# Attention and MoE in one kernel: the order of an attention unit's work on four engines taken from a table of beats

## The chip, the core and the metric

The kernel runs on one NeuronCore of a Trainium2 chip. Its engines each have an in-order queue of their own: PE (TensorE, matrix products), DVE (VectorE), ACT (ScalarE), POOL (GpSimd) and SP (SyncE, which here only issues DMAs). The metric is the device time of one launch in microseconds (us).

## What is computed

```python
scores = scale * q @ k.T                      # (4, 8, 576, 576), head_dim 64
x = log1p(abs(pos_i - pos_j)) / log1p(max(pos_i, 1))
bias = relu(x[..., None] @ w1 + b1) @ w2       # hidden 32, 8 heads
a = scores + bias - max
a = exp(a); a = a / (a.sum(-1) + 1e-9)
x = (a @ v).transpose(0, 2, 1, 3).reshape(2304, 512)
h = x @ w_in                                   # 512 x 2048
g = where(h >= 1, h, where(h <= -1, 0, (h + 1)**2 / 4))
out = g @ w_out
```

Everything is fp32. The kernel gets that precision from products of a high part (a value rounded to fp32r) and a low part (the rest): of each product of two matrices it keeps high x high, low x high and high x low.

## The kernel before

There are three stages. The first builds the bias, 36 groups of 16 query rows, and writes it to DRAM (`steps`, `sums`, `combine`). The third is the MoE part, three blocks of 768 tokens, which waits for hardly anything but PE. Between them lies the attention, which the change is about.

**A unit** is one batch element and one pair of heads: 4 pairs x 4 batch elements make 16 units, n = 0 to 15. Queries come in four blocks of 128 (k = 0 to 3) and a last one (L) that holds the remaining 64 queries of both heads. For each block:

- PE computes scores S for both heads (12 products, line 429) into two PSUM tiles of two banks each. The pool `psS` has two such tiles, so the tiles of one block must be read before the next block's products can start.
- DVE adds the bias, negates and finds the row extreme in one instruction per head, written to e (line 457, 475 for L); this frees S.
- ACT takes the exponential in place and leaves the row sum in `sum` (line 464).
- PE transposes e in 128 x 128 pieces (line 432) into a PSUM tile T; tiles T come from a pool of four (`psT`), which also holds the outputs O and R.
- The transposed tile is split into hi and lo. Plain tiles: ACT rounds to hi, DVE subtracts for lo (lines 493, 494). For five of the eight tiles of a unit (`POOL` in `CFG`) ACT copies T to SBUF (c, line 498), hi is made by DVE from T (three of them, line 502) or by POOL from c (two, line 500), and POOL subtracts (line 503). Keys 512 to 575 of both heads share a tile (T_s, `shared`).
- PE multiplies the values by hi (5 products) and by lo (5 products) into O (line 429, `values`), ACT copies O out, SP stores it.

The row sums go: ACT adds eps, DVE takes the reciprocal of the 128 x 9 tile `sum` (line 629), PE transposes it into a tile R of its own (line 542), ACT copies it out (line 544), SP stores it. The reciprocals multiply x later, when the MoE part's activations are prepared.

**Preparation.** While unit n runs, unit n+1's q, k and v are loaded and split: DVE rounds kh (line 163) and vs (line 174), POOL subtracts (line 136). The pool of vs has two tiles, so vs of unit n+1 is written over that of unit n-1. Some units also prepare an activation tile of the first MoE block (`XQ`: load, add and multiply on DVE, lines 383 and 384, round on ACT, subtract on POOL) or a weight tile (`WQ`: units 5, 6, 9 and 10).

**The order** is that of the emitting loop: for each unit and block, the scores, a slot for preparation work (`step`), then an entry of `GAPS`, which holds transposes of the block before and output products of this unit or the one before:

```python
GAPS = (
    ((av, 1, 0, 1), (tr, 1, 4)),
    ((tr, 0, 0), (av, 1, 1, 0)),
    ((tr, 0, 1), (av, 1, 1, 1)),
    ((tr, 0, 2),),
    ((tr, 0, 3), (av, 0, 0, 0)),
)
```

`tr, 0, k` transposes block k of the current unit, `av, back, half, j` makes O of a unit `back` units earlier. Instructions that pass through `keep` stay in the order of the program on their engine; the others (most of DVE's and ACT's of the attention) a scheduler may move.

Of the kernel before, what the change touches and what calls it, by code (L numbers as in the profile page):

```python
# [32 lines left out]
CFG = dict(un=[('paaa', 'paav')[g in (1, 30, 32, 34)] for g in range(NG)], bb=5, mv=1, hi='pvvpv', rb='a', pool=((0, 1), (2, 0), (2, 1), (3, 0), (3, 1)), sb=4, keep=1, drain=2, diag='a', rb2='v', eps='v', rc=2, rbb=1, hb=2, rawb=(2, 2), t=(3, 11, 10, 18, 11, 12, 19), eb=4, seq=0, pb=(6, 9, 12, 14, 16), pq=22, tb=6, ub=12, low0='ppp', anch=(8, 8, 16, 23, 23), low1='ppp', ob=4, gb=4, fin=2, lastp=15, xs=2, sbf=('v', 'v', 'v', 'v', 'v'), bsE=(), ytail='p')  # L33
EPS = 1e-9
RB = 2
LASTP = CFG["lastp"]
FIRST = ((0, 3), (1, 5), (2, 33))
XQ = {(0, 0): (39, "raw", 43), (1, 0): (79, "raw", 83), (2, 0): (118, "raw", 123), (3, 0): (137, "bias", 142),
      (0, 1): (125, "x", 136), (1, 1): (131, "raw", 145), (2, 1): (139, "x", 151), (3, 1): (148, "raw", 155)}
WQ = {(0, 0): (49, 53), (0, 1): (59, 63), (1, 0): (89, 93), (1, 1): (99, 103)}  # L40
LB = ((1, 1), (2, 1), (3, 2), (3, 3), (2, 3))
POOL, SB, KEEP, RBB = CFG["pool"], CFG["sb"], CFG["keep"], CFG["rbb"]
STEPS = sorted((t, i) for i, t in enumerate(CFG["t"]))
# [5 lines left out]
def attn_cpb_moe_kernel(ctx, tc, qk, vL, cb, win, wout, lw, ident, ii, out):  # L49
# [27 lines left out]
    last_y, stored, narrow = [], [], []  # L77
# [71 lines left out]
    def prep(n):  # L149
# [4 lines left out]
        def high(ins):  # L154
            if n == 1:
                keep(ins)
            else:
                early(ins)
# [6 lines left out]
        def load_r():  # L165
            a["r"] = lp.tile([P, KQ], F32, tag="qk", name=f"qk{n}", bufs=CFG["rawb"][0])
            with ExitStack() as after:
                if n == 2:
                    after.enter_context(tc.issue_after(narrow[0].ins))
                nc.sync.dma_start(out=a["r"], in_=qk[n])  # L170
# [5 lines left out]
        def load_v():  # L176
            a["rv"] = lp.tile([P, 10, D], F32, tag="v", name=f"v{n}", bufs=CFG["rawb"][1])
            with ExitStack() as after:
                if n == 2:
                    after.enter_context(tc.issue_after(narrow[0].ins))  # L180
                nc.sync.dma_start(out=a["rv"].rearrange("p a b -> p (a b)"), in_=vL[n])

        def part(i):


            def f():
                if i == 0:
# [198 lines left out]
    def split_x(k, j, home):  # L386
# [15 lines left out]
        return scaled, high, rest  # L402

    with ExitStack() as ph:
# [8 lines left out]
        def load_bias(p, k):  # L413
# [8 lines left out]
            else:  # L422
                t = bp.tile([P, S], F32, tag="biasL", name=f"biasL{p}", bufs=2)
                for j in range(2):
                    narrow[:] = [nc.sync.dma_start(out=t[D * j : D * j + D, :], in_=bias_r[4][:, 2 * p + j, :])]
# [8 lines left out]
        def scores(n, k, qkv, bias):  # L434
            kh, kl = qkv["h"][:, :KW], qkv["l"][:, :KW]
            qh, ql = qkv["h"][:, KW:], qkv["l"][:, KW:]
            parts_ = ((qh, kh), (ql, kh), (qh, kl))
            if k == 0:
                sums[n] = stp.tile([P, 9], F32, tag="sum", name=f"sum{n}", bufs=3)
            later = []  # L440
            sm = sums[n]
            mx = stp.tile([P, 2], F32, tag="mx", name=f"mx{n}_{k}", bufs=6)
            if k < 4:
                e = ep.tile([P, 2 * S], F32, tag="e", name=f"e{n}_{k}")
                pss = [psS.tile([P, 2, 512], F32, tag="S", name=f"S{n}_{k}_{j}") for j in range(2)]
                for hf in range(2):
                    for i, (q_, k_) in enumerate(parts_):
                        for j in range(2):
# [3 lines left out]
                                pss[j][:, hf, :HS], q_[d, P * k : P * k + P], k_[d, kc : kc + HS],  # L452
                                start=i == 0, stop=i == 2, tile_position=(D * j, 0),
                            )
                for j, ps in enumerate(pss):
                    ev = e[:, S * j : S * j + S]
                    nc.vector.tensor_tensor_reduce(  # L457
                        out=ev.rearrange("p (a b) -> p a b", a=2),
                        in0=ps[:, :, :HS],
                        in1=bias[k][:, S * j : S * j + S].rearrange("p (a b) -> p a b", a=2),  # L460
                        scale=-0.125, scalar=BIG, op0=ALU.add, op1=ALU.min, accum_out=mx[:, j : j + 1],
                    )
                    later.append(
                        lambda ev=ev, j=j: nc.scalar.activation(  # L464
                            ev, ev, AF.Exp, bias=mx[:, j : j + 1], scale=-1.0, accum_out=sm[:, 4 * j + k : 4 * j + k + 1]
                        )
                    )
            else:
                e = ep.tile([P, S], F32, tag="eL", name=f"e{n}_L", bufs=2)
                ps = psS.tile([P, 2, 512], F32, tag="S", name=f"S{n}_L")  # L470
                for hf in range(2):
                    kc = D + HS * hf
                    for i, (q_, k_) in enumerate(parts_):
                        pe_mm(ps[:, hf, :HS], q_[:, 512:QW], k_[:, kc : kc + HS], start=i == 0, stop=i == 2)
                nc.vector.tensor_tensor_reduce(
                    out=e.rearrange("p (a b) -> p a b", a=2), in0=ps[:, :, :HS],
                    in1=bias[4].rearrange("p (a b) -> p a b", a=2),
                    scale=-0.125, scalar=BIG, op0=ALU.add, op1=ALU.min, accum_out=mx[:, 0:1],
                )
                def last():  # L480
                    y = nc.scalar.activation(e, e, AF.Exp, bias=mx[:, 0:1], scale=-1.0, accum_out=sm[:, 8:9])
                    for j in range(2):
                        h_ = slice(D * j, D * j + D)
                        nc.scalar.copy(diag[n % 2][h_, h_], e[h_, 512:S])
                    nc.scalar.activation(sm, sm, AF.Identity, bias=eps_s)
                    return y

                later.append(last)
            return e, later

        def split(ps, hi, lo, e=None, kj=None):
            if e is None:
                nc.scalar.copy(hi, ps)  # L493
                nc.vector.tensor_tensor(out=lo, in0=ps, in1=hi.bitcast(F32), op=ALU.subtract)  # L494
            else:
                c = sp.tile([P, 512], F32, tag="c4", name="c4", bufs=SB)
                m = c.rearrange("p (a b) -> p a b", a=4) if len(hi.shape) == 3 else c[:, : hi.shape[1]]
                nc.scalar.copy(m, ps)  # L498
                if CFG["hi"][POOL.index(kj)] == "p":
                    pool(nc.gpsimd.tensor_copy(hi, m))  # L500
                else:
                    nc.vector.tensor_copy(hi, ps)  # L502
                r = nc.gpsimd.tensor_tensor(out=lo, in0=m, in1=hi.bitcast(F32), op=ALU.subtract)  # L503
                pool(r)

        def EV(n, k, j):
            return nc.gpsimd if (k, j) in POOL and n < LASTP else None

        def transposes(n, k, es, eT):
            hi, lo = eT  # L510
            off = P * (k % 2)
            e = es[k]
            if k < 4:
                for j in range(2):
                    ps = psT.tile([P, 4, P], F32, tag="T", name=f"T{n}_{k}_{j}")
                    for tb in range(4):
                        c0 = 640 * j + P * tb
                        pe_tr(ps[:, tb, :], e[:, c0 : c0 + P], id_s)
                    split(ps, hi[:, 4 * j : 4 * j + 4, off : off + P], lo[:, 4 * j : 4 * j + 4, off : off + P], EV(n, k, j), (k, j))
            else:  # L520
# [26 lines left out]
        def values(n, half, j, eT, vs):  # L547
# [13 lines left out]
            if j == 0:  # L561
                return
# [521 lines left out]
```

## Time and profile before

| | us |
|---|---|
| median of 3 runs | 756.23 |
| range of the runs | 755.06 to 756.64 |
| the profiled execution | 756.44 |
| its span in the profile | 754.6 |
| PE busy | 703.7 (93% of the span) |
| DVE, ACT, POOL busy | 532.6, 518.3, 506.6 |
[...]

The span runs from the first to the last instruction; the execution's own time is 1.8 us more. PE counts as busy from a product's start to its modelled end, and products overlap in the pipeline, so a start-to-start distance says more than a sum of durations. A row of the timeline that merges several instructions gives the start of the first, the time to the end of the last and their count (x). What stands in brackets at a row's end is idle time just before it and what ended it.

### The profile page before, as it was taken

The numbers are of one execution on the slowest core, as the hardware profiler recorded it, in microseconds if no ns is written. First come the engines' busy times: TensorE is split into PE (matmuls) and PEld (weight loads), VectorE is DVE, ScalarE is ACT, GpSimd is POOL, SyncE is SP. The second block draws the span as 40 slices with busy tenths as digits, with TensorE's granted clock in tenths as the row PEclk, the third lists the DMA queues.
The fourth block names the chain that finished last, engine by engine and source line by source line (L and its number), as shares of the span: only waits on it lengthen the run. The fifth ranks groups of instructions, "written<-read, shape, count | busy, mean of one in ns | idle before, by whom it ended". The sixth has DMA issues, their size and how long they took to land.

```text
span 754.6 us, 14003 instructions
## 1 busy us (share of the span) xinstructions
PE 703.7 (93%) x4864; PEld 601.9 (80%) x4864; DVE 532.6 (71%) x1043; ACT 518.3 (69%) x1156; POOL 506.6 (67%) x422
## 2 busy tenths in 40 slices
PE   5677999899999999889999999999999999999997
PEld 2234788787888888778988889898989988888886
DVE  7998887888778888885867687354455465666563
ACT  8996888888888988776646465444444447666663
POOL 7986766777887887751757768665647555665662
PEclk9998999999999999999999999999999999999999
DMA  6688444733553464334354655033021002000002
GB/s 190 207 270 240 148 134 130 250 113 118 171 167 112 117 196 130 96 92 137 107 175 148 180 166 173 2 116 87 9 57 39 1 0 85 1 1 0 1 2 83
DMA packets 51239, 83.98 MB, mean 111 GB/s; under 512 B 11216, under 2 KB 31456, under 8 KB 51168
## 3 DMA queue, kind: packets, MB, share of 16 engines
q1 hardware_dynamic: 50880, 82.87, 35.8%
q8 instruction: 38, 0.62, 0.3%
q14 instruction: 33, 0.27, 0.1%
q10 hardware_dynamic: 288, 0.22, 0.1%
HBM read 57.95 MB, written 25.12 MB: 110 GB/s over the span
## 4 chain that ended last, share of the span: by engine, by line
PE 57%; DVE 11%; ACT 11%; DMA 4%; issue 4%; POOL 3%; SPq 2%; DVEq 0%; ACTq 0%; POOLq 0%
PE y L692 20%; PE h L692 12%; PE p L692 7%; PE O L429 7%; PE S L429 6%; PE T L432 4%; ACT e L464 4%; DVE e L457 2%; ACT c L498 2%; DVE lo L494 1%; SPq L378 1%; DMA raw<-in_wout_dram 1%; ACT hi L493 1%; DVE x L383 1%; DVE w L116 1%
## 5 line engine op out<-in xcount | busy, mean ns | idle before, releaser
L934 POOL TENSOR_TENSOR gl<-c,gh 128x384 fp32r<-128x384 f32 x64 | 70.2, 1098 | 109.0 <-issue 88.0
L503 POOL TENSOR_TENSOR lo<-c,hi 128x512 fp32r<-128x512 f32 x75 | 104.7, 1413 | 52.4 <-DVE hi L502 50.0
L692 PE MATMUL y<-w1h,gl 128*128 128x512 f32 x288 | 114.0, 396 | 0.0
L692 PE MATMUL y<-w1l,gh 128*128 128x512 f32 x288 | 113.7, 395 | 0.0
L464 ACT ACTIVATE e<-e,mx 128x576 f32<-128x576 f32 x128 | 99.1, 781 | 19.3 <-DVE mx L457 19.3
L692 PE MATMUL y<-w1h,gh 128*128 128x512 f32 x288 | 112.0, 389 | 0.0
L457 DVE CUSTOM_DVE_ANT_0 e<-S,bias 128x576 f32<-128x576 f32 x128 | 92.5, 751 | 12.5 <-PE S L429 11.7
L432 PE MATMUL T<-id_s,e 128*128 128x128 f32 x512 | 75.0, 285 | 10.6 <-ACT e L464 8.3
L752 ACT ACTIVATE c<-c,half_s 128x384 f32<-128x384 f32 x64 | 39.4, 616 | 61.6 <-DVE c L749 61.6
L432 PEld LDWEIGHTS T<-id_s,e 128*128 128x128 f32 x512 | 55.6, 143 | 26.6 <-ACT e L464 20.5
L958 POOL TENSOR_TENSOR gl<-c,gh 128x384 fp32r<-128x384 f32 x32 | 32.8, 1025 | 47.8 <-issue 22.3
L692 PEld LDWEIGHTS y<-w1h,gl 128*128 128x128 f32 x288 | 54.0, 187 | 11.5
L271 ACT ACTIVATE u<-lw,nthr 128x576 f16<-128x576 f32 (+17 forms) x104 | 57.5, 647 | 4.3 <-DVE lw L236 2.4
L692 PEld LDWEIGHTS y<-w1l,gh 128*128 128x128 f32 x288 | 54.0, 187 | 8.0
L692 PEld LDWEIGHTS y<-w1h,gh 128*128 128x128 f32 x288 | 54.1, 188 | 7.7
L429 PE MATMUL O<-hi,vs 128*128 128x256 f32 (+1 forms) x320 | 58.3, 312 | 0.7 <-DVE lo L494 0.6
L290 PEld LDWEIGHTS <-qh 128*32 128x32 f16 x704 | 19.5, 101 | 47.7 <-issue 24.4
L273 POOL TENSOR_SCALAR u<-lw,thr 128x576 f16<-128x576 f32 (+17 forms) x36 | 51.8, 1453 | 7.6 <-DVE lw L236 3.9
L749 DVE TENSOR_SCALAR c<-h 128x384 f32<-128x384 f32 x64 | 35.3, 552 | 27.0 <-PE h L692 25.2
L930 ACT CAST gh<-c 128x384 fp32r<-128x384 f32 x64 | 32.9, 514 | 31.3 <-DVE c L755 30.1
L755 DVE TENSOR_TENSOR c<-h,c 128x384 f32<-128x384 f32 x64 | 35.5, 554 | 26.4 <-ACT c L752 25.6
L429 PE MATMUL O<-lo,vs 128*128 128x256 f32 (+1 forms) x320 | 53.0, 296 | 0.0
(264 smaller groups left out, 2051.7 us busy)
## 6 DMA issues: line engine op xcount, KB each, us to landing
bias_d<-y SPq DMA_DIRECT2D x36, 295.5 KB, 4.5
qk<-in_qk_dram SPq DMA_DIRECT2D x16, 640.0 KB, 5.4
x<-xT SPq DMA_DIRECT2D x48, 192.0 KB, 3.3
raw<-in_win_dram SPq DMA_DIRECT2D x16, 512.0 KB, 5.8
raw<-in_wout_dram SPq DMA_DIRECT2D x16, 512.0 KB, 3.9
v<-in_vL_dram SPq DMA_DIRECT2D x16, 320.0 KB, 2.8
bias<-bias_d SPq DMA_DIRECT2D x16, 288.0 KB, 4.6
out_dram<-o SPq DMA_DIRECT2D x17, 256.0 KB, 2.1
```

The costliest lines, as they stand in the source:

```text
L271: tc.keep_in_program_order(nc.scalar.activation(u[:, :n_], lw1[:, :n_], AF.Sigmoid, bias=nthr[:, m : m + 1], scale=STEEP))
L273: EN[x].tensor_scalar(out=u[:, :n_], in0=lw1[:, :n_], scalar1=thr[:, m : m + 1], scalar2=None, op0=ALU.is_gt)
L429: keep(nc.tensor.matmul(*a, **k))
L432: keep(nc.tensor.transpose(*a))
L457: nc.vector.tensor_tensor_reduce(out=ev.rearrange("p (a b) -> p a b", a=2), in0=ps[:, :, :HS], in1=bias[k][:, S * j : S * j + S].rearrange ...
L464: lambda ev=ev, j=j: nc.scalar.activation(ev, ev, AF.Exp, bias=mx[:, j : j + 1], scale=-1.0, accum_out=sm[:, 4 * j + k : 4 * j + k + 1])
L503: r = nc.gpsimd.tensor_tensor(out=lo, in0=m, in1=hi.bitcast(F32), op=ALU.subtract)
L692: a = nc.tensor.matmul(out, w, x, start=start, stop=stop)
L749: keep(nc.vector.tensor_scalar(out=c, in0=h, scalar1=-1.0, scalar2=1.0, op0=ALU.max, op1=ALU.min))
L752: keep(nc.scalar.activation(c, c, AF.Square, scale=0.5, bias=half_s))
L755: keep(nc.vector.tensor_tensor(out=c, in0=h, in1=c, op=ALU.max))
L934: keep(nc.gpsimd.tensor_tensor(out=gl, in0=c, in1=gh.bitcast(F32), op=ALU.subtract))
```

## The change

The loop over `GAPS`, the scheduler's freedom and the counters go. Each piece of a unit's work gets a name and a time, its beat, in the table `BEAT`; a unit starts every 15.5 beats (`UNIT`). All pieces of all units are put into one list, sorted by beat, and emitted in that order, and every instruction passes through `keep`: the order on PE, DVE, ACT and POOL is the table's. Beside that:

- Four tiles go over POOL instead of five, ((0,0), (0,1), (1,1), (2,0)), and POOL makes hi of all four; DVE makes none.
- The two halves of T_L are split as one tile.
- The products of values by hi and by lo are separate pieces (`O10h`, `O10l`), between which other work may stand.
- The row sums are transposed raw, into the corner of the tile T_s of the second half; ACT adds eps as it copies the 9 x 128 result out, and DVE takes the reciprocal there, on 9 partitions of 128 elements. R has no tile of its own any more.
- The last unit uses POOL too, and the loads of q, k and v follow the table alone, without the order that held unit 2's behind the bias loads.

```diff
+UNIT = 15.5
+BEAT = {
+    "load_r": -26.3, "load_v": -13.9, "kh": -9.4, "kl0": -6.4, "vh": -5.9, "kl1": -4.7, "vl": 3.6,
...
+    "O01l": 17.7, "l31": 18.4, "lL": 19.0, "c01": 19.5, "Ts1": 19.6, "hs1": 20.3, "R": 20.6, "O10h": 20.9,
...
+        def on(n, t, f, *a):
+            events.append((UNIT * n + t, len(events), f, a))
...
+            def transpose_shared(half):
+                ps = psT.tile([P, 512], F32, tag="T", name=f"T{n}_s{half}")
+                for i in range(2):
+                    pe_tr(ps[:, P * i : P * i + P], e[2 * half + i][:, 512:640], id_s)
+                if half:
+                    pe_tr(ps[:9, 384:512], sm, id_s)
+                    pe_mm(ps[:, 256:320], diag[n % 2], ii_s, start=True, stop=True)
...
+            def low_(key):
+                ps, hi, lo = tr[key]
+                if key in POOL:
+                    keep(nc.gpsimd.tensor_copy(hi, ps))
+                    keep(nc.gpsimd.tensor_tensor(out=lo, in0=ps, in1=hi.bitcast(F32), op=ALU.subtract))
+                else:
+                    keep(nc.vector.tensor_tensor(out=lo, in0=ps, in1=hi.bitcast(F32), op=ALU.subtract))
+
+            def sums_out():
+                r = out["r"] = sp.tile([9, P], F32, tag="r", name=f"r{n}")
+                keep(nc.scalar.activation(r, out["sum"], AF.Identity, bias=eps_s[:9]))
+
+            def inverse():
+                r = out["r"]
+                keep(nc.vector.reciprocal(out=r, in_=r))
+                nc.sync.dma_start(out=rT[p][b].rearrange("(k q) -> k q", q=P), in_=r)
+
+            def values(half, j, part):
...
+                ps, src = out[half, j], eT[half][part]
+                for i in range(5):
+                    tb = 4 * j + i if i < 4 else 8
+                    pe_mm(ps[:, :w], vs[:, 8 + j if i == 4 else tb, :], src[:, tb, :], start=part == i == 0, stop=part == 1 and i == 4)
...
+        while events:
+            i = min(range(len(events)), key=lambda i: events[i][:2])
+            _, _, f, a = events.pop(i)
+            f(*a)
```

What the table does to the queues shows at two places that the prediction speaks of. First PE, between the scores of blocks 2 and 3 of unit 2 and its last scores (O1 is the output of unit 1, T2 the transposes of unit 2, `x4` that a row stands for four products; of the 12 products of S2_3 only the first is shown). Before:

```order
L432 MATMUL T2_1_0_2109<-id_s_143,e2_1_2032 128x128 x4
L432 MATMUL T2_1_1_2116<-id_s_143,e2_1_2032 128x128 x4
L432 MATMUL T2_s0_2123<-id_s_143,e2_0_1978 128x128
L429 MATMUL O1_1_1_2130<-hi1_1_1905,vs1_1679 128x320 x5
L429 MATMUL O1_1_1_2130<-lo1_1_1906,vs1_1679 128x320 x5
L432 MATMUL R1_2142<-id_s_143,sum1_1717 9x128
L429 MATMUL S2_3_0_2149<-kh2_1736 128x288
L432 MATMUL T2_2_0_2170<-id_s_143,e2_2_2092 128x128 x4
L432 MATMUL T2_2_1_2179<-id_s_143,e2_2_2092 128x128 x4
L429 MATMUL S2_L_2193<-kh2_1736 128x288
```

Now, on the same stretch of PE:

```order
L434 MATMUL T2_1_0_2086<-id_s_143,e2_1_2005 128x128 x4
L431 MATMUL O1_1_0_2056<-lo1_1_1906,vs1_1639 128x320 x5
L434 MATMUL T2_1_1_2102<-id_s_143,e2_1_2005 128x128 x4
L434 MATMUL T2_s0_2109<-id_s_143,e2_0_1960 128x128
L431 MATMUL S2_3_0_2117<-kh2_1809 128x288
L431 MATMUL O1_1_1_2139<-hi1_1_1905,vs1_1639 128x320 x5
L431 MATMUL O1_1_1_2139<-lo1_1_1906,vs1_1639 128x320 x5
L434 MATMUL T2_2_0_2157<-id_s_143,e2_2_2066 128x128 x4
L434 MATMUL T2_2_1_2165<-id_s_143,e2_2_2066 128x128 x4
L431 MATMUL S2_L_2175<-kh2_1809 128x288
```

The last output product of the unit before, O1_1_1, stood ahead of the scores of block 3 and now stands behind them; the low half of O1_1_0 has moved in between the transposes; R is gone.

Second DVE, around the rounding of vs for unit 3 (a row e, mx is the maximum of one head; r is the reciprocal; the brackets name the engines and DMA queues that a row waits for). Before:

```order
L494 TENSOR_TENSOR lo2_0_2055<-T2_s0_2123,hi2_0_2054 128x256 [waits Activation_49]
L174 CAST vs3_2201<-v3_2027 128x10x64 [waits DMAHW6_49,PE_49]
L457 ISA e2_3_2148,mx2_3_2147<-S2_3_0_2149,bias0_3_1519 128x576 [waits DVE_49,PE_49]
L457 ISA e2_3_2148,mx2_3_2147<-S2_3_1_2150,bias0_3_1519 128x576 [waits PE_49]
L502 CAST hi2_1_2168<-T2_2_0_2170 128x4x128 [waits DVE_49,Activation_49,Pool_49]
```

Now:

```order
L544 TENSOR_TENSOR lo1_1_1906<-T1_s1_2029,hi1_1_1905 128x320 [waits PE_49,Activation_49]
L171 CAST kh3_2063<-qk3_1790 128x1280 [waits DMAHW5_49]
L552 RECIPROCAL r1_2054<-r1_2054 9x128
L457 ISA e2_2_2066,mx2_2_2065<-S2_2_0_2067,bias0_2_1515 128x576 [waits DVE_49,PE_49]
L457 ISA e2_2_2066,mx2_2_2065<-S2_2_1_2068,bias0_2_1515 128x576 [waits PE_49]
L544 TENSOR_TENSOR lo2_0_2041<-T2_1_0_2086,hi2_0_2040 128x4x128 [waits DVE_49,Activation_49]
L179 CAST vs3_2133<-v3_1986 128x10x64 [waits DMAHW6_49,PE_49]
L457 ISA e2_3_2116,mx2_3_2115<-S2_3_0_2117,bias0_3_1519 128x576
L457 ISA e2_3_2116,mx2_3_2115<-S2_3_1_2118,bias0_3_1519 128x576
L544 TENSOR_TENSOR lo2_0_2041<-T2_s0_2109,hi2_0_2040 128x256 [waits Activation_49]
```

vs of unit 3 is still ahead of the two maxima of block 3 and still waits for PE, which must have finished with vs of unit 1, so with O1_1_1. The maxima behind it wait for PE no more by themselves: what vs waits for comes later than their scores. The rounding of kh and the reciprocal now stand ahead of the maxima of block 2.

## Rows read from the trace of the kernel before

**Rows 1.** Stretches: us, then busy us (instructions) of PE, PEld, DVE, ACT, POOL
```profile
68.28:352.03 283.75, 262.04 (x2195) 228.55 (x2195) 229.82 (x521) 239.40 (x623) 202.46 (x160) 0.99 0.48 146
352.03:754.60 402.57, 395.92 (x1967) 353.85 (x1966) 241.45 (x394) 218.69 (x427) 244.26 (x212) 1.00 0.22 68
114.48:131.17 16.69, 15.91 (x140) 14.08 (x138) 12.93 (x32) 14.44 (x39) 12.64 (x10) 1.00 0.33 101
131.17:148.75 17.58, 16.08 (x139) 14.11 (x137) 14.78 (x34) 14.84 (x40) 14.11 (x11) 1.00 0.79 251
148.75:166.77 18.02, 16.25 (x139) 14.10 (x137) 14.70 (x34) 16.16 (x42) 13.91 (x11) 1.00 0.41 137
184.81:200.87 16.06, 15.91 (x138) 14.07 (x138) 12.83 (x32) 13.91 (x38) 12.63 (x10) 1.00 0.37 103
```

**Rows 2.** PE timeline (start, us, what): last scores of first and last unit
```profile
80.84 0.38 PE L429 MATMUL S_L<-kh 128*128 128x288 f32 x1
...
342.40 0.40 PE L429 MATMUL S_L<-kh 128*128 128x288 f32 x1
```

**Rows 3.** Waits, 100 to 340 us: us in total, times, longest
```profile
PEld T L432 <- ACT e L464: 15.8, 39, 0.9
...
PE R L432 <- DVE lo L494: 5.9, 7, 1.3
```

**Rows 4.** Timeline of PE through one unit, 184.8 to 201 us
```profile
185.92 1.41 PE L432 MATMUL T<-id_s,e 128*128 128x128 f32 x8
...
187.08 0.84 PE L429 MATMUL O<-hi,vs 128*128 128x256 f32 x5
...
190.74 0.60 PE L432 MATMUL T_L<-id_s,e_L 128*128 128x128 f32 x4
...
191.66 0.40 PE L429 MATMUL S<-kh 64*128 64x288 f32 x2
...
197.21 0.98 PE L429 MATMUL O<-hi,vs 128*128 128x320 f32 x5
...
198.76 0.27 PE L432 MATMUL R<-id_s,sum 128*9 128x128 f32 x1
...
198.96 0.40 PE L429 MATMUL S<-kh 64*128 64x288 f32 x2
...
199.72 0.30 PE L429 MATMUL S<-ls,kh 64*128 64x288 f32 x2
...
199.96 1.09 PE L432 MATMUL T<-id_s,e 128*128 128x128 f32 x8
...
200.87 0.40 PE L429 MATMUL S_L<-kh 128*128 128x288 f32 x1
```

**Rows 5.** Timeline of DVE, 184 to 203 us
```profile
187.23 0.84 DVE L163 CAST kh<-qk 128x1280 fp32r<-128x1280 f32 x1
...
192.88 0.48 DVE L494 TENSOR_TENSOR lo<-T_s,hi 128x320 fp32r<-128x320 f32 x1
...
199.14 0.48 DVE L174 CAST vs<-v 128x640 fp32r<-128x640 f32 x1
...
200.05 0.76 DVE L457 CUSTOM_DVE_ANT_0 e<-S,bias 128x576 f32<-128x576 f32 x1 [0.43 <-PE S L429]
...
200.73 0.75 DVE L457 CUSTOM_DVE_ANT_0 e<-S,bias 128x576 f32<-128x576 f32 x1
```

**Rows 6.** Line views of two reciprocals: xcount: min/median/max ns, starts; shapes
```profile
L244 DVE RECIPROCAL rsc<-m x1: 164/164/164, 6.6 to 6.6; 128x1 f32<-128x1 f32 x1
...
L629 DVE RECIPROCAL sum<-sum x16: 199/215/217, 86.4 to 347.3; 128x9 f32<-128x9 f32 x16
```

**Rows 7.** DVE timeline beside an activation tile (142 us), a weight (162 us)
```profile
142.54 1.20 DVE L383 TENSOR_TENSOR x<-x 128x384 f32<-128x384 f32 x1
...
144.55 0.75 DVE L457 CUSTOM_DVE_ANT_0 e<-S,bias 128x576 f32<-128x576 f32 x1
...
162.16 1.23 DVE L116 SCALAR_TENSOR_TENSOR a<-a,raw 128x512 int32<-128x512 int32 x1
...
163.92 0.41 DVE L121 CAST w0h<-a 128x512 fp32r<-128x512 f32 x1
```

**Rows 8.** Timeline of POOL while the bias is built
```profile
20.37 3.05 POOL L136 TENSOR_TENSOR ls<-qk,kh 128x640 fp32r<-128x640 f32 x2
```

More of the change, by code (lines that the diff above doesn't have):

```diff
@@ L154, in high @@
         def high(ins):
[L155 to L158, printed above, removed]
+            keep(ins)
         def high_k():
@@ L166, in load_r @@
             a["r"] = lp.tile([P, KQ], F32, tag="qk", name=f"qk{n}", bufs=CFG["rawb"][0])
[L167 to L170, printed above, removed]
+            nc.sync.dma_start(out=a["r"], in_=qk[n])
         def high_v():
@@ L432, in pe_tr @@
             keep(nc.tensor.transpose(*a))
[L434 to L445, printed above, removed]
+        N = NP * B
@@ L451, in scores @@
                             pe_mm(
-                                pss[j][:, hf, :HS], q_[d, P * k : P * k + P], k_[d, kc : kc + HS],
+                                sc[k, j][:, hf, :HS], q_[d, P * k : P * k + P], k_[d, kc : kc + HS],
                                 start=i == 0, stop=i == 2, tile_position=(D * j, 0),
                             )
[L455 to L513, printed above, removed]
-                for j in range(2):
[L515 to L520, printed above, removed]
+            def maxima(k, j):
+                most(e[k][:, S * j : S * j + S], sc[k, j], bias[p][k][:, S * j : S * j + S], mx[k][:, j : j + 1])
@@ new lines, in attn_cpb_moe_kernel, with load_b @@
+        for n in range(N):
+            if n > 1:
+                preps[n] = prep(n)
+            if n:
+                for x, f in zip(("load_r", "load_v", "kh", "vh", "kl0", "kl1", "vl"), preps[n]):
+                    on(n, BEAT[x], f)
+            on(n, BEAT["S0"] - 0.01, unit, n)
+        for p in range(1, NP):
+            bias[p] = {}
+            for k, (b, k_) in enumerate(LB):
+                def load_b(p=p, k=k):
+                    bias[p][k] = load_bias(p, k)
+                on(B * (p - 1) + b, 3.1 * k_ + 0.5, load_b)
@@ L610, in step @@
-        def step(i_):
-            store_x()
-            for f in jobs.pop(10 * n + i_, ()):
-                f()
-            for m in range(3):
-                for t, i in STEPS:
-                    if t == 20 - 10 * m + i_ and 0 < n + m < N:
-                        preps[n + m][i]()
-        go[0] = True
-        def tr(n, k):
-            half = k // 2 if k < 4 else 1
-            if k in (0, 2):
-                w = 256 + D * half
-                eT[n, half] = [(tp0, tp1)[half].tile([P, 9, w], F32R, tag=f"{x}{half}", name=f"{x}{n}_{half}") for x in ("hi", "lo")]
-            transposes(n, k, es[n], eT[n, half])
-            if k in (1, 4):
-                shared(n, half, es[n], eT[n, half])
-            if k == 4:
-                nc.vector.reciprocal(out=sums[n], in_=sums[n])
```

255 lines of the change are left out of this document (132 added, 123 removed), and 9 rows, old and new, of the table BEAT.

## The prediction

> **What bounds the kernel.** I read the stretches first. The attention, from the first scores to the first product of the MoE part, takes 283.75 us, and PE is busy for 262.04 of them; the MoE part takes 402.57 with PE busy for 395.92 [rows 1]. The change leaves the MoE part's own work as it is, so what can be won lies in PE's waits inside the attention. Its pitch is the distance between the last scores of two units: from 80.84 to 342.40 us there are 15 pitches in 261.56 us, 17.44 each [rows 2]. They are not alike. The stretches of single units run from last scores to last scores: 16.69 for a unit with nothing beside it, 17.58 for one with an activation tile, 18.02 for one with a weight, and 16.06 for a unit that follows heavy ones; PE is busy 15.9 to 16.25 in each, ACT 13.9 to 16.2, DVE 12.8 to 14.8 [rows 1]. The waits say what PE lacks: its weight loads for transposes waited 15.8 us for exponentials, and the transposed row sums 5.9 us for DVE [rows 3]. Everyone is nearly full and everyone waits a little, as in-order queues do that hand small pieces to each other.
>
> **What PE needs.** In the 16.06 us unit PE was idle for 0.15, and the eight transposes at 185.92 took 1.16 to the next start, where the same eight at 199.96 take 0.91 [rows 4]: a need of 16.06 - 0.15 - 0.25 = 15.66 us. The change keeps all of PE's products, so this is the floor of the new pitch.
>
> **What the new order makes wait.** Let scores of block 3, S3, start at 0. PE passes on after 1.00 (198.96 to 199.96); DVE's first maximum starts at 1.09 (200.05), its second 0.68 later (200.73), and PE's next scores 0.14 after that (200.87) [rows 4, 5]. Ten output products on 320 columns take 1.55 (197.21 to 198.76). Now:
>
> - After S3 PE runs O1_1 of the unit before (to 2.55) and two transposed tiles (to 3.46), then the last scores, which need the first PSUM tile of S3 free.
> - DVE's queue has vs ahead of that tile's maximum, and vs waits for the end of O1_1, seen by DVE some 0.09 after PE passes on: 2.64. vs takes 0.48 [rows 5], the maximum 0.68, the release 0.14: 3.94.
>
> PE thus waits 3.94 - 3.46 = 0.48, and the pitch is 15.66 + 0.48 = 16.14. Queued behind vs are both maxima of block 3, and behind those ACT's two exponentials; the maxima start 3.12 instead of 1.09 after S3, 2.03 later. The transposes of block 3 come after the last scores (1.00 more of PE) and the first finds its exponential done, so the wait for exponentials goes, and this one takes its place.
>
> **The reciprocal.** From 128 x 1 to 128 x 9 elements it goes from 164 to 215 ns [rows 6], 6.4 ns per element; on 9 x 128 that is 164 + 127 x 6.4 = 980 ns (bounds: 0.22 as in the row, and 1.01 from the row's longest; I take the slope, since both rows are of one operation). It stands ahead of the maxima of block 2. Let S1 start at 0: maxima from 1.09 to 2.45, lo 0.48, kh 0.85, reciprocal 0.98, two maxima 1.36, release 0.14 [rows 5]: 6.26. PE comes to S3 at: S1 1.00, the shared tile 0.47 (0.92 from 190.74 to 191.66, less four transposes at 0.45), raw sums 0.20, transposes 0.91, half an output 0.78, S2 1.00, transposes 0.91, the other half 0.78, the small shared tile 0.23: 6.28 [rows 4]. It just fits: cost nothing, and 0.02 us of cover. [...] No row of this case shows a reciprocal longer than 9 elements.
>
> **Heavy units.** An activation tile costs DVE 2.01 us (142.54 to 144.55), a weight 1.23 + 0.41 = 1.64 [rows 7]. Both now stand between block 3's maxima and the last maximum. After S3, counted as above, DVE is through the second maximum at 4.48, through a lo of 256 columns (0.4, by the 0.48 for 320 [rows 5]) at 4.9; with the tile 6.9, then the last maximum 0.68 and its release: 7.7. PE wants that tile for the next unit's scores at 7.17: 16.14 less the way from S0 to S3, which is S0 1.00, four transposes 0.45, ten products on 256 columns 1.24 (four fifths of 1.55) and the 6.28 above, 8.97. So 0.55 for each of units 4, 8, 12, 13, 14, and for a weight 0.2 to 0.4, say 0.3, in units 6, 7, 9, 10. Unit 15 has two more tiles ahead of its last scores, no vs and no kh: some 0.5.
>
> **Costed at nothing.** DVE loses three roundings per unit, ACT one small instruction and one of two pieces of T_L, and POOL trades one subtraction for two roundings: DVE has at least 2.8 us idle in each unit shown and POOL at least 3.4 [rows 1], so neither sets the pitch; without that cover each 0.1 us a unit would be 1.5 us. The load of q and k for unit 2 now stands in SP's queue among the bias stores and waits for POOL's subtractions, over at 23.42 [rows 8]; stores behind it come up to 2.5 us late, under six y buffers. The end of unit 15 has the same chain as before (last scores, maximum, exponential, transposes, outputs) with POOL's four pieces done by then: 0, within -1 and +2.
>
> **The sum.** 15 x 16.14 = 242.1; + 5 x 0.55 + 4 x 0.3 + 0.5 = 246.6, against 261.6: -15.0. The profiled execution took 756.44, 0.2 above the median: 741.4; I say 741.5.
>
> **The rivals.**
>
> - *The wait for vs is hidden* (0.15). If maxima follow O1_1 sooner, or PE's transposes last longer, the pitch is 15.66; with nothing for heavy units 234.9, so 729.7. For it: PE was idle 0.15 in the best unit. Against: the wait is in the queue for certain, only its size is not.
> - *A light unit stays at 16.69* (0.17), because handovers that I put at 0.1 cost 0.2 to 0.3 in each of some five places. 15 x 16.69 + 4.45 = 254.8: 749.7. For it: light units of before are above their floor by 1.0 with waits as small.
> - *The reciprocal outgrows its cover* (0.06). Two rows of 1 and 9 elements bear an extrapolation to 128 badly, and its cover is 0.02 us. [...]
> - *Slower: ACT becomes the bound* (0.06). Block 3's exponentials stand in ACT's queue ahead of two copies and two roundings, and all of it now waits 2.03 us longer. If ACT idles for all of that, a unit takes what ACT is busy, plus 2.03: light 16.5, activation 16.9 + 0.55, weight 18.2. With six light units, five and four: 99 + 87 + 73 = 259, 753.8. Each 0.1 more is 1.5 us, so it is slower from a wait of 2.3 on (O1_1 late by 0.3, say, for its lo); at 2.6 it is 762. Against: ACT has 1.9 to 2.7 us idle a unit now [rows 1], and other work of the same unit lies ahead of the exponentials.
> - *No change* (0.04): PE's order is the old one but for some moves, and what is won in one place is lost in another.
>
> **How the numbers follow.** My forecast, pitches of 16.0 to 16.4 and 737 to 746 us, has 0.52. Two runs of this kernel differ by up to 0.2%, 1.5 us, so faster is under 754.7. Faster: 0.52 + 0.15 + 0.17 + 0.06 = 0.90; same 0.04; slower 0.06. The range leaves out the last two rivals, 0.10, and takes in the others with their ends: 729.7 and 749.7, so 730 to 750.
>
> **What would show it.** Right: a pitch near 16.1 between last scores, PE waiting about 0.5 us for the maximum just before them, DVE idle some 2 us ahead of vs, waiting for O; the reciprocal near 1 us; waits for exponentials nearly gone; the MoE part 402 us long as before. Wrong: pitches of 16.7 or more, PE waiting at other places (transposes of the last block, O1_0), or ACT without gaps.

## The result

| | us | runs |
|---|---|---|
| before, beside it | 756.43 (755.06 to 756.74) | 4 |
| changed | 745.88 (744.71 to 746.77) | 4 |
| ratio | 0.9863, 95% interval 0.9844 to 0.9882 | |
| forecast | 741.5, range 730 to 750 | |

The change is faster by 10.6 us; 15 were forecast. The profiled execution took 745.66 us, its span is 743.5.

### The profile after

Stretches of the changed kernel, columns as in [rows 1]: attention, MoE part, then one unit alone, one with an activation tile, one with a weight, each from last scores to last scores.

```profile
68.21:342.27 274.06, 263.08 (x2196) 230.80 (x2197) 212.12 (x471) 234.67 (x591) 211.75 (x185) 0.99 0.47 145
342.27:743.50 401.23, 395.15 (x1966) 353.62 (x1964) 239.87 (x394) 218.70 (x426) 243.69 (x212) 1.00 0.22 70
113.56:130.28 16.72, 16.19 (x138) 14.23 (x138) 12.30 (x29) 14.19 (x37) 12.31 (x12) 1.00 0.54 168
147.00:164.13 17.13, 16.25 (x138) 14.21 (x138) 13.62 (x31) 14.59 (x38) 13.84 (x13) 1.00 0.37 123
180.84:197.58 16.74, 16.19 (x138) 14.23 (x138) 13.54 (x31) 15.24 (x39) 14.09 (x13) 1.00 0.64 200
```

Against [rows 1] the attention lost 9.7 us and the MoE part 1.3. The light unit stands where it stood (16.69, now 16.72). The heavy ones came down: 17.58 to 17.13 with an activation tile, 18.02 to 16.74 with a weight. The last scores of the first and the last unit are at 80.09 and 332.50: 252.41 us in place of 261.56 [rows 2], where 246.6 were forecast. So the gain lies in pitches that were heavy before, and nearly half of it in the last two, up to unit 15: 19.53 and 18.70 before, 17.14 and 16.64 now.

Waits between 100 and 330 us (in total, times, longest):

```profile
...
DVE vs L179 <- PE O L431: 28.6, 13, 2.2
ACT e L454 <- DVE mx L457: 27.5, 23, 2.0
DVE lo L544 <- ACT r L548: 10.5, 14, 0.8
...
PE S_L L431 <- DVE mx L457: 6.2, 13, 0.5
PEld S L431 <- DVE mx L457: 5.4, 19, 0.5
...
PEld T L434 <- ACT e L454: 2.5, 13, 0.2
```

The wait of PE's transposes for exponentials fell from 15.8 [rows 3] to 2.5, and the one for vs came, both as forecast. Two rows were not: DVE's lo waits for r, ACT's copy of the raw row sums, and ordinary scores S wait for maxima. The timeline of PE through the light unit (start, us, what) shows where:

```profile
112.04 1.04 PE L434 MATMUL T<-id_s,e 128*128 128x128 f32 x8
113.56 0.37 PE L431 MATMUL S_L<-kh 128*128 128x288 f32 x1 [0.48 <-DVE mx L457]
...
114.57 0.62 PE L434 MATMUL T<-id_s,e 128*128 128x128 f32 x4
...
125.75 0.85 PE L431 MATMUL S<-kh 64*128 64x288 f32 x2
...
127.19 1.00 PE L431 MATMUL O<-hi,vs 128*128 128x320 f32 x5
128.03 0.90 PE L431 MATMUL O<-lo,vs 128*128 128x320 f32 x5
128.76 1.04 PE L434 MATMUL T<-id_s,e 128*128 128x128 f32 x8
130.28 0.37 PE L431 MATMUL S_L<-kh 128*128 128x288 f32 x1 [0.48 <-DVE mx L457]
```

Block 3's scores at 125.75 take 1.44 to the next start, since the second head waits for its PSUM tile; they took 1.00 in [rows 4]. And the eight transposes ahead of the last scores take 1.52 to the next start. DVE and the engines it meets, in the timeline of all engines of the same kernel:

```profile
122.40 0.34 ACT L548 ACTIVATE r<-T_s,eps_s 9x128 f32<-9x128 f32 x1
122.78 0.49 DVE L544 TENSOR_TENSOR lo<-T_s,hi 128x320 fp32r<-128x320 f32 x1 [0.71 <-ACT r L548]
...
123.92 0.93 DVE L552 RECIPROCAL r<-r 9x128 f32<-9x128 f32 x1
...
125.98 3.10 POOL L147 TENSOR_TENSOR ls<-qk,kh 128x640 fp32r<-128x640 f32 x2
...
128.96 0.49 DVE L179 CAST vs<-v 128x640 fp32r<-128x640 f32 x1 [2.21 <-PE O L431]
...
129.37 0.75 DVE L457 CUSTOM_DVE_ANT_0 e<-S,bias 128x576 f32<-128x576 f32 x1
130.05 0.75 DVE L457 CUSTOM_DVE_ANT_0 e<-S,bias 128x576 f32<-128x576 f32 x1
```

DVE stands idle for 2.21 us until it can begin vs, and both maxima of block 3 are behind vs. The low part of the shared tile waits 0.71 for r, which stands in the table (R, 20.6) behind an exponential; kh, the reciprocal and block 2's maxima follow it, and they release the PSUM tile that block 3's scores want.

### The profile page after: what moved, and what is told of

The parts are those of the page before. It is cut to its first block, busy times and chain, and to the rows that moved or that the text cites. A ratio compares the mean times of both kernels' runs of the same rounds, so it can differ in the third digit from the quotient of the medians.

```text
span 743.5 us, 14025 instructions
## 1 busy us (share of the span) xinstructions
PE 704.1 (95%) x4864; PEld 603.9 (81%) x4864; DVE 513.3 (69%) x993; ACT 513.6 (69%) x1124; POOL 512.3 (69%) x445
## 4 chain that ended last, share of the span: by engine, by line
PE 55%; ACT 10%; DVE 8%; POOL 7%; issue 6%; DMA 4%; SPq 1%; DVEq 0%; POOLq 0%; ACTq 0%
PE y L672 23%; PE h L672 15%; PE p L672 7%; PE O L431 4%; PE S L431 3%; POOL lo L542 3%; ACT e L454 2%; DVE e L457 2%; PE T L434 2%; ACT hi L536 2%; POOL ls L147 2%; POOL hi L541 1%; DMA bias<-bias_d 1%; DVE r L552 1%; DMA x<-rT 1%
## 5 line engine op out<-in xcount | busy, mean ns | idle before, releaser
L457 DVE CUSTOM_DVE_ANT_0 e<-S,bias 128x576 f32<-128x576 f32 x128 | 90.8, 744 | 8.5 <-PE S L431 5.6
L542 POOL TENSOR_TENSOR lo<-c,hi 128x512 fp32r<-128x512 f32 x64 | 83.6, 1307 | 5.1
L541 POOL CAST hi<-c 128x512 fp32r<-128x512 f32 x64 | 48.4, 757 | 56.1 <-ACT c L533 56.1
L434 PEld LDWEIGHTS T<-id_s,e 128*128 128x128 f32 x512 | 59.3, 144 | 6.5 <-issue 3.2
L431 PE MATMUL S<-kh 64*128 64x288 f32 x256 | 53.3, 349 | 3.7 <-DVE mx L457 2.2
```

What stands on the lines that cost most here:

```text
L431: keep(nc.tensor.matmul(*a, **k))
L434: keep(nc.tensor.transpose(*a))
L457: keep(nc.vector.tensor_tensor_reduce(out=o.rearrange("p (a b) -> p a b", a=2), in0=ps[:, :, :HS], in1=of.rearrange("p (a b) -> p a b", a= ...
L541: keep(nc.gpsimd.tensor_copy(hi, ps))
L542: keep(nc.gpsimd.tensor_tensor(out=lo, in0=ps, in1=hi.bitcast(F32), op=ALU.subtract))
```

## The experiments

Each time is a median with its ratio to runs of the kernel before on the same chip. "Light" is the usual pitch of a unit with nothing beside it, from last scores to last scores.

| run | us | ratio (95%) | light |
|---|---|---|---|
| changed | 745.88 | 0.9863 (0.9844 to 0.9882) | 16.72 |
| e1_vs_later | 731.90 | 0.9674 (0.9661 to 0.9687) | 15.79 |
| e2_sums_earlier | 743.42 | 0.9839 (0.9824 to 0.9854) | 16.69 |
| e3_both | 729.31 | 0.9637 (0.9618 to 0.9656) | 15.39 |
| e4_before_pool | 749.78 | 0.9909 (0.9896 to 0.9923) | 16.7 |
| e5_port_free | 744.01 | 0.9839 (0.9825 to 0.9853) | 16.58 |
| e6_one_piece | 730.88 | 0.9662 (0.9647 to 0.9678) | 15.75 |
| e7_prep_first | 778.03 | 1.0287 (1.0273 to 1.0302) | 16.7 |
| e8_best | 730.11 | 0.9662 (0.9644 to 0.9679) | 15.39 |
| e9_port_free2 | 743.17 | 0.9830 (0.9817 to 0.9844) | 16.27 |
| e10_best2 | 727.43 | 0.9627 (0.9613 to 0.9642) | 15.37 |
| e11_order_only | 801.81 | 1.0598 (1.0581 to 1.0614) | none alike |
| e12_third_buffer | 730.91 | 0.9664 (0.9651 to 0.9678) | 15.79 |

### Two waits, alone and together: e1, e2, e3

```diff
-"vh": -5.9      +"vh": -3.6       (e1, e3: vs behind block 3's maxima)
-"R": 20.6       +"R": 20.35       (e2, e3: r directly behind hs1 on ACT, the rounding of the shared tile)
```

> Edit: the rounding of the values of the next unit (vs) alone moves behind the row maxima of block 3 on VectorE. Theory (two waits in a row stand on TensorE's path in every unit: 0.48 us at S_L, because the rounding of vs waits for the products O1_1 of the unit before and holds the maxima back, and 0.46 us at the second head of S3, because ls1 waits 0.72 us for ScalarE's copy of the row sums): the wait at S_L goes, the one at S3 stays, pitch of a light unit 16.72 - 0.48 = 16.24 us, fifteen pitches -7.2, time about 739 us. Rival A (the pitch is a loop through ScalarE, whose exponentials and copies just fill it): the wait turns up again at another product, pitch 16.6 to 16.72, time 744 to 746. Rival B (the vs rounding is now late for the values' products O0 of the next unit): a new wait there, time above 746.

> Edit: ScalarE's copy of the row sums stands directly behind hs1, ahead of the exponentials of block 1's first head; nothing else moves. Theory (two waits in a row): ls1 no longer waits for the copy (0.72 us now), so kh, the reciprocal, the maxima of block 2 and the second head of S3 come about 0.46 us sooner, pitch 16.72 - 0.46 = 16.26, time about 739 us. Rival A (a loop through ScalarE): the exponentials behind the copy come 0.34 us later, nothing is gained, pitch 16.7 or more, 745 to 748 us. Rival B (the wait at S_L takes up what S3 gives back, because vs still waits for O1_1 of the unit before, and that is what sets the pitch): the wait at S_L grows from 0.48 to 0.9, time 745 to 746.

> Both edits: the rounding of vs behind the maxima of block 3, and the copy of the row sums directly behind hs1. Theory (two separate waits in a row): their gains add up, pitch 15.75 to 15.9 us (the products alone need 15.66), fifteen pitches -12 to -14, time 732 to 734 us. If one of the two set the pitch alone, the time is that of the better single edit, 738 to 740. Rival A (ScalarE's own work sets the pitch): within 2 us of 746.

e1 went to 731.90, further than the theory's 739; e2 to 743.42, a little under the 745 to 746 of Rival B but with its wait of 0.90 at the last scores; e3 to 729.31, a little below the sum forecast for it. The timeline of PE in e3 is the unit without waits:

```profile
94.66 0.38 PE L431 MATMUL S_L<-kh 128*128 128x288 f32 x1
...
106.70 0.40 PE L431 MATMUL S<-kh 64*128 64x288 f32 x2
...
107.69 1.00 PE L431 MATMUL O<-hi,vs 128*128 128x320 f32 x5
...
109.26 1.04 PE L434 MATMUL T<-id_s,e 128*128 128x128 f32 x8
110.05 0.38 PE L431 MATMUL S_L<-kh 128*128 128x288 f32 x1
...
110.93 0.27 PE L434 MATMUL T<-id_s,e 128*128 128x128 f32 x1
```

Its light unit takes 15.39. Laid beside it, the changed kernel's loses 0.73 between the eight transposes and the last scores (1.52 against 0.79), 0.13 in the last scores themselves (1.01 against 0.88) and 0.45 in block 3's scores (1.44 against 0.99): 16.70, measured 16.72. So the row's "0.48" of idle time stands for 0.86 of pitch: the bracket counts from the modelled end of the transposes, whose 1.04 overlap the next start where nothing waits. e1 takes the first item away and keeps the second (15.79 - 15.39 = 0.40).

In e2 the second item goes, and the first grows by nearly as much. The timeline of all engines in e2 says why:

```profile
124.80 0.40 PE L431 MATMUL S<-kh 64*128 64x288 f32 x2
...
125.04 3.09 POOL L147 TENSOR_TENSOR ls<-qk,kh 128x640 fp32r<-128x640 f32 x2
...
125.79 1.00 PE L431 MATMUL O<-hi,vs 128*128 128x320 f32 x5
...
127.56 0.92 DVE L179 CAST vs<-v 128x640 fp32r<-128x640 f32 x1 [2.51 <-PE O L431]
128.08 0.87 POOL L541 CAST hi<-c 128x512 fp32r<-128x512 f32 x1
...
129.30 0.37 PE L431 MATMUL S_L<-kh 128*128 128x288 f32 x1 [0.90 <-DVE mx L457]
```

Counted from block 3's scores, O1_1 comes sooner (0.99 us behind them, 1.44 in the changed kernel) and POOL's ls does not (0.24 and 0.23), so vs now starts in the middle of a subtraction and takes 0.92 us for the work of 0.49: it ends at 128.48, 0.35 behind POOL's second subtraction (125.04 + 3.09 = 128.13).

### Is it POOL that makes vs long? e5, e9

```diff
-"kl0": -6.4     +"kl0": -6.65     (e5, e9, on top of e2: half of ls ahead of tile (0,0) on POOL)
-"vl": 3.6       +"vl": -2.8       (e9: POOL's next work needs vs itself, so POOL stands still beside it)
```

> Edit: e2_sums_earlier, and on GpSimd the first half of ls (the low part of the next unit's keys and queries) stands ahead of the rounding and low part of tile (0,0) instead of behind them, so that GpSimd's subtractions should end just before the rounding of vs begins. Theory formed from e2 (the pitch is a loop: exponentials of block 3, ScalarE's row of work, the copy of tile (0,0), GpSimd's rounding, subtraction and both halves of ls, and the rounding of vs on VectorE, which does not run beside a subtraction on GpSimd and ends 0.35 us behind it whatever its own start; then the maxima and the exponentials of block 3 again): the rounding of vs takes 0.4 to 0.5 us instead of 0.92, the wait at S_L falls from 0.9 to about 0.45, pitch 16.70 - 0.45 = 16.25, time 743.4 - 7 = 736 to 737 us. Rival A (ScalarE's own row of work sets the pitch and GpSimd has nothing to do with it): pitch 16.7, time 743 to 744. Rival B (GpSimd's part (0,0) comes too late for O00): a new wait at O00, time over 744.

e5 missed: 744.01. The edit didn't do what it was to do, as its timeline of all engines shows:

```profile
128.56 0.61 POOL L541 CAST hi<-c 128x512 fp32r<-128x512 f32 x1
128.70 0.81 DVE L179 CAST vs<-v 128x640 fp32r<-128x640 f32 x1 [2.50 <-PE O L431]
```

The subtraction was over, but POOL's next rounding had just begun, and vs ended 0.34 behind that one. It was 0.11 shorter than in e2, and the light pitch 0.11 shorter.

> Edit: e5_port_free, and on GpSimd the low part of the next unit's values, which needs the rounding of vs, stands directly behind the second half of ls. GpSimd then waits for that rounding and has nothing else running beside it (in e5 the rounding of tile (0,1) had begun there, and vs took 0.81 us and ended 0.34 us behind it). Theory (in e2 and e5 the rounding of vs is as long as what GpSimd has begun before it, and each 0.1 us of it is 0.1 us of pitch): vs takes 0.42 to 0.49 us, light pitch 16.58 - 0.35 = 16.2 to 16.25, fifteen pitches -5, time 738 to 740 against 744.0. Rival A (the length of the rounding is not GpSimd's doing, or the pitch is not set by it): pitch 16.55 to 16.6, 743 to 745. Rival B (GpSimd's tiles (0,1) and (1,1) are now 1.6 us later and too late for O01): over 745.

The timeline of all engines of e9:

```profile
128.57 0.49 DVE L179 CAST vs<-v 128x640 fp32r<-128x640 f32 x1 [2.52 <-PE O L431]
...
129.15 1.56 POOL L147 TENSOR_TENSOR vs<-v,vs 128x640 fp32r<-128x640 f32 x1 [0.69 <-DVE vs L179]
...
129.89 0.37 PE L431 MATMUL S_L<-kh 128*128 128x288 f32 x1 [0.48 <-DVE mx L457]
```

Nothing runs on POOL beside vs: 0.49 again, and the light pitch is 16.27, 0.88 above e3's, as the theory has it. The whole came to 743.17 all the same, since heavy units rose to 17.14, weight units from 16.69 in e2: there the preparation on DVE now meets POOL's moved work, and its two instructions beside a weight take 1.13 and 1.40 us in place of 0.77 and 0.72 (medians of lines 127 and 132). The theory holds for the unit; the time that I forecast for the kernel does not.

### Is it the wait for O1_1 or the place of vs? e12

```diff
-a["v"] = qp.tile([P, 10, P], F32R, tag="vs", name=f"vs{n}")
+a["v"] = qp.tile([P, 10, P], F32R, tag="vs", name=f"vs{n}", bufs=3)
```

> Edit: the changed kernel, order untouched, with three buffers in place of two for the rounded values vs; its rounding then needs no longer wait for the products O1_1 of the unit before. Theory (it is that wait, not the place of the rounding ahead of the maxima, that costs 0.87 us in each unit at the scores S_L): the rounding falls into the 2.2 us that VectorE stands still ahead of it, the wait at S_L goes, the one at the second head of S3 (0.44) stays, pitch 15.39 + 0.44 = 15.8, time about 732 us as in e1_vs_later. Rival (the rounding meets GpSimd's two subtractions of ls there, which lasted 3.1 us, and ends behind them all the same): the wait at S_L stays, pitch above 16.5, 742 to 746 us.

730.91, light pitch 15.79, as in e1 with the order untouched. The timeline of all engines:

```profile
123.82 0.81 PE L431 MATMUL S<-kh 64*128 64x288 f32 x2
124.00 3.34 POOL L147 TENSOR_TENSOR ls<-qk,kh 128x640 fp32r<-128x640 f32 x2
...
124.72 1.20 DVE L179 CAST vs<-v 128x640 fp32r<-128x640 f32 x1
...
127.58 0.38 PE L431 MATMUL S_L<-kh 128*128 128x288 f32 x1
```

vs meets POOL here as well and takes 1.20, but it starts 0.90 us after block 3's scores and not 3.21 (128.96 less 125.75 in the changed kernel), so nobody waits for it. With two buffers a tile that is written for the next unit hangs on the last reader of the unit before; the wait for O1_1 is shown as the cause, by its removal in two ways.

### The heavy units: e4, e7, e8, e10, e11

e4 gives the kernel before POOL's new tiles and no other part of the change:

```diff
-hi='pvvpv', ... pool=((0, 1), (2, 0), (2, 1), (3, 0), (3, 1))
+hi='pppp', ... pool=((0, 0), (0, 1), (1, 1), (2, 0))
```

> The kernel before with one part of the change alone: the tiles that GpSimd rounds and splits are (0,0), (0,1), (1,1), (2,0) as after, and the order is left to the old planner, which plans with the new assignment. Theory (the gain of the change is the order of the heavy units, above all the maxima ahead of the preparation work on VectorE): no gain, 752 to 760 us. Rival (the gain is VectorE relieved of roundings and GpSimd of a tile): 744 to 750 us.

The rival: 749.78, 6.8 us under the kernel before, without the table. The old planner makes another order of it, so this is assignment and replanning together. e11 is the reverse, the table with the old tiles, three of them rounded by DVE where the table has their copies:

```diff
-pool=((0, 0), (0, 1), (1, 1), (2, 0))
+pool=((0, 1), (2, 0), (2, 1), (3, 0), (3, 1))
...
+if key in ((2, 0), (2, 1), (3, 1)):
+    keep(nc.vector.tensor_copy(hi, ps))
...
```

> Edit: the changed kernel with its table of beats, but with the tiles of the kernel before on GpSimd ((0,1), (2,0), (2,1), (3,0), (3,1)), of which VectorE rounds three as before. With e4_before_pool (the assignment alone, 749.8 us) this makes two by two: order and assignment apart. Theory (after e4: in the old order the assignment alone was worth 6.8 of 10.5 us; with the table the assignment matters as well, since VectorE gets three roundings of about 0.6 us more and GpSimd a subtraction more): 750 to 760 us, most of the gain of the change gone. Rival (the order is what counts, any assignment goes with it): 744 to 748.

It took 801.81, far above both. Its waits name the new neighbours:

```profile
POOL lo L545 <- DVE hi L536: 72.8, 17, 6.1
...
PE T L434 <- DVE lo L547: 23.2, 12, 1.9
```

POOL's subtractions wait for roundings that the table put behind other work on DVE. So order and assignment can't be priced apart by swapping one: each order needs its own tiles. How much of the 10.6 us each brings stays open, and the change's smaller parts (T_L as one tile, raw row sums, POOL in the last unit) were not tried by themselves.

e7 moves the preparation on DVE ahead of block 3's maxima, behind vs:

```diff
-enumerate((0, 0.9, 2.4, 3.4))          +enumerate((-2.2, -2.1, 2.4, 3.4))
-zip((7.0, 9.3, 12.4, 13.3, 15.8), fs)  +zip((7.0, 9.3, 10.2, 10.3, 15.8), fs)
```

> Edit: the changed kernel, in which the preparation for the experts on VectorE (two instructions of an activation or weight tile, in units 4 and 6 to 10 and 12 to 15) goes ahead of the row maxima of block 3, behind the rounding of vs, instead of behind those maxima. Theory (what made the heavy units cheap is that the maxima are ahead of the preparation): 1.5 to 2 us directly on the loop in each of nine heavy units, less the 0.41 that five of them pay now: 11 to 14 us slower than the changed kernel, 757 to 760. Rival (the order within VectorE matters little, the heavy units are cheap because VectorE has fewer roundings): under 3 us slower, 746 to 749.

778.03: the theory's direction, and more than its 757 to 760. The timeline of all engines beside a weight, and the stretch from 180 to 280 us:

```profile
202.84 0.49 DVE L179 CAST vs<-v 128x640 fp32r<-128x640 f32 x1 [2.19 <-PE O L431]
...
203.25 1.10 DVE L127 SCALAR_TENSOR_TENSOR a<-a,raw 128x512 int32<-128x512 int32 x1
203.88 1.59 POOL L542 TENSOR_TENSOR lo<-c,hi 128x512 fp32r<-128x512 f32 x1
204.38 1.37 DVE L132 CAST w1h<-a 128x512 fp32r<-128x512 f32 x1
...
206.57 0.37 PE L431 MATMUL S_L<-kh 128*128 128x288 f32 x1 [2.90 <-DVE mx L457]
...
207.60 1.07 PE L434 MATMUL T<-id_s,e 128*128 128x128 f32 x4
...
208.32 0.56 PE L431 MATMUL O<-hi,vs 128*128 128x256 f32 x1
```

```profile
180.00:280.00 100.00, 85.43 (x673) 76.49 (x670) 71.05 (x146) 74.22 (x185) 67.61 (x59) 0.91 0.46 141
```

The two instructions take 2.4 us in place of some 1.5 beside POOL's, and PE waits 2.90 at the last scores in place of 0.48. A weight unit grew by more than that, from 16.73 to 20.47: the transposes and the ten output products right behind those last scores took 3.00 where the changed kernel's take 1.66 (the first four transposes 0.72 to the next start, 207.60 to 208.32, and 0.38 there, 198.59 to 198.97). The clock granted to TensorE from 206 to 213 us, behind the pause, is 0.76 of full speed; in the 100 us shown it is 0.91, and in e3 from the first last scores to the last 1.00. In this table it is the place of the maxima ahead of the preparation that keeps heavy units cheap.

e8 and e10 add to e3 a later place for the preparation, behind the last block's maxima; e10 also puts ACT's rounding of an activation tile behind the last exponentials.

```diff
-enumerate((0, 0.9, 2.4, 3.4))          +enumerate((1.7, 1.8, 2.4, 3.4))   (e8; e10: 3.0, 3.9 at the end, two tiles of unit 15 left)
-zip((7.0, 9.3, 12.4, 13.3, 15.8), fs)  +zip((7.0, 9.3, 12.4, 14.15, 15.8), fs)
```

> Edit: e3_both, and the preparation's instructions on VectorE that stood between the maxima of block 3 and those of the last block (for a weight tile the rounding alone, for an activation tile both) go behind the maxima of the last block. Theory: in e3 nine heavy units have a pitch of 15.80 to 15.87 against 15.39 of the light ones, because the maxima of the last block wait for these instructions (a weight's rounding there takes 1.40 us instead of 0.72, since it stands beside a subtraction on GpSimd); that wait goes, nine times 0.45 = 4 us: 725 us, all pitches 15.39 to 15.5. Rival (TensorE's products or the exponentials are late for another reason in these units): no gain, 728 to 730.

> Edit: e3_both, and as in e8_best the rounding of a weight tile and both VectorE instructions of an activation tile behind the maxima of the last block; but ScalarE's rounding of the activation tile now stands behind the exponentials of the last block (in e8 it stood ahead of them, waited 1.25 us for VectorE and held them back), and the one activation tile with a place of its own stays. Theory: weight units 15.38 to 15.65 as in e8, activation units 15.4 to 15.6 instead of 15.80; eight or nine units times 0.4, 3 to 4 us: 725.5 to 726.5 against 729.3. Rival (the tile T_L or the exponentials behind come late all the same): activation units 15.8 or more, 728 to 730.

Weight units fell as expected, from 15.8 to between 15.38 and 15.64. Activation units did not: 16.14 and more in e8 (17.98 at the last, where the two other tiles of unit 15 moved as well), 15.82 to 15.89 in e10, against 15.80 to 15.85 in e3. e8's timeline beside an activation tile:

```profile
143.85 0.85 DVE L394 TENSOR_TENSOR x<-x,xr 128x384 f32<-128x384 f32 x1
144.74 0.52 ACT L398 CAST xh<-x 128x384 fp32r<-128x384 f32 x1 [1.25 <-DVE x L394]
145.16 0.77 ACT L454 ACTIVATE e_L<-e_L,mx 128x576 f32<-128x576 f32 x1
```

ACT waits for DVE ahead of the exponential that T_L needs; in e10 the rounding comes behind it, and T_L's weight loads then wait for that rounding, 2.8 us in six places. e8 took 730.11 and e10 727.43, both more than expected (725, and 725.5 to 726.5); e10's is the lowest of the study, 3.7% under the kernel before; their intervals overlap that of e3, so what e10 adds to e3 is not settled.

### The halves: e6

```diff
-"ls1": 21.3, "O10l": 23.3     +"ls1": 20.85, "O10l": 20.95   (on top of e3)
```

> Edit: e3_both with the products O10 in one piece: the half that multiplies the low parts (O10l) directly behind the half that multiplies the high parts, ahead of the scores of block 2, and the low part of the shared tile emitted ahead of it (VectorE's order stays). This prices the halves alone where no other wait is left. Theory: S2 and with it the maxima of block 2 come 0.81 us later; the maxima now start directly behind the reciprocal, with some 0.4 us to spare, so the second head of S3 waits 0.2 to 0.4 us in each unit: 732 to 735 us against 729.3. Rival A (the products are covered by the transposes anyway): 728 to 730, the halves are worth nothing. Rival B (the low part of the shared tile comes late for O10l and TensorE waits for it as well): over 738.

730.88, under the 732 to 735 expected. By time it can't be told from e3's 729.31 (intervals overlap); by the profile the light pitch is 15.75, 0.36 longer, as the theory said, while heavy units stay at 15.8. The halves are worth 0.36 in a light unit, once nothing else is in the way.

## Why the prediction was right, and where it was not

The sign and the range held, the range partly by luck: the pitch of a light unit came out at 16.72, which the prediction itself had named as a sign of being wrong (16.7 or more), and cheaper heavy units made up part of it. Nothing of the gain forecast for light units (16.69 to 16.14) came. Step by step:

- **Where the time lies.** Right: the MoE part moved by 1.3 us, from 402.57 to 401.23.
- **What PE needs, 15.66.** 0.27 too long: e3 runs at 15.39. The unit it was read from lost more than the 0.15 of idle time and the one slow group of transposes: its last scores take 1.11 to the next start (184.81 to 185.92 in that timeline) and e3's 0.88, its other groups of eight transposes 0.85 to 0.93 and e3's 0.79 to 0.80.
- **The wait for vs.** The mechanism was right in every link (vs ahead of the maxima, held by O1_1, DVE idle 2.2 us ahead of it), and e1 and e12 show it by taking it away. Its price was not: 0.86, not 0.48. From PE passing on from O1_1 to the last scores the sum had 0.09 + 0.48 + 0.68 + 0.14 = 1.39; the rows give 0.20 + 0.41 + 0.68 + 0.23 = 1.52. The transposes meanwhile last 0.79 and not 0.91, and the last scores themselves go 0.13 slower after the pause.
- **The step that failed: the way to block 3's scores.** The sum let lo start directly behind block 1's maxima, and all of DVE's chain just fit. But lo starts when r is done, 0.7 us later, and PE loses 0.45 at the second head. No term had it: r is in the prediction only as ACT's "one small instruction", under what is costed at nothing, and what stands behind it was not followed. Together: 16.14 - 0.27 + 0.38 + 0.45 = 16.70. The forecast's 15 pitches were 8.7 us too short by this. The rival that let a light unit stay at 16.69 had the number but not the cause: not five handovers of 0.2, two waits.
- **The reciprocal.** 0.98 was extrapolated, 0.93 is in the rows. It did not outgrow its cover: with lo on time (e3) block 3's scores wait for nothing behind it. From the 215 ns for 9 elements [rows 6] to the 932 for 128 (median of line 552 in the changed kernel) it is 6.0 ns per element; the slope taken was 6.4.
- **Heavy units.** Forecast 0.55 and 0.3 above a light unit, 4.45 us in all; measured 0.41 for four of the activation tiles and nothing for weights, 1.6 us. This made up 2.8 of the 8.7 us. Why they were cheaper than forecast is not shown. In e3, where PE comes sooner, both cost 0.41 to 0.48, but there the preparation on DVE also meets POOL: a weight's rounding takes 1.40 us in place of 0.72 (line 132), an activation tile's addition 1.53 in place of 0.85 (line 394).
- **The rest.** Start and end of the attention gave 0.5 us and the MoE part 1.3, where nothing was put down. 8.7 - 2.8 - 1.8 makes up the 4 us between forecast and profiled execution.
- **Slower by ACT.** Did not come: ACT does wait for block 3's maxima, up to 2.0 us and 27.5 in all, but PE's chain was longer.
- **The hidden wait.** Its 729.7 is what e3 reaches, with two numbers of the table altered, but by luck: e3's pitch is 0.27 under the rival's, and its longer units, for which the rival puts down nothing, add 4.3 us.

## What to carry to other kernels

Before an instruction is put early into an in-order queue, ask which old reader its buffer waits for: behind it the whole queue stands, and a third buffer or a place behind the urgent work took the wait away here (light pitch 16.72, then 15.79 in e12 and in e1). An idle time in a row's bracket is not the price of a wait (0.48 here, and 0.86 of pitch); lay the unit beside one that doesn't wait and compare start to start. When one wait is removed and the time stays, look whether the piece that came sooner has run into another engine, as vs did in e2 (0.92 us, ending 0.35 behind POOL's subtraction).

## What the runs showed of the hardware

DVE's rounding of vs, SBUF to SBUF, took longer beside POOL's roundings and subtractions. It takes 0.49 us with POOL still (e9). Where it began during an instruction of POOL's, it ended 0.34 to 0.36 us behind that instruction in three runs: it took 0.92 in e2, 0.81 in e5, and 1.20 in e12 (where POOL's first subtraction from 124.00, put at the 1.56 that is its median in the changed kernel, ends at 125.56 and vs at 125.92). POOL's work was longer as well: its rounding of a tile took 0.87 in e2, where it began during vs, and 0.61 in e5, where it came first; its two subtractions took 3.34 in e12 with vs beside them from 0.72 us on, and 3.09 in e2 and 3.10 in the changed kernel, where vs began in their last 0.57 and 0.12. In e7 preparation and POOL's work beside it are both longer: DVE's two instructions 1.10 and 1.37 (0.78 and 0.72 in the changed kernel), POOL's subtraction 1.59 (median there 1.29). What lengthens them was not shown.

lo of the shared tile starts when ACT's r is done (122.40 + 0.34 = 122.74 in the changed kernel, then 122.78), though both only read the same PSUM tile; why one waits for the other was not tried, only that an earlier r takes the wait off DVE's path.
